# Seven half-size products in place of eight for the first channel product of a token-and-channel mixer

## The chip, the cores and the metric

The kernel runs on one core of one Trainium2 chip. A core has a matrix engine (TensorE, PE in the profile, with the loading of its weights shown apart as PEld), a vector engine (VectorE, DVE), an engine for functions of one argument (ScalarE, ACT), a general engine (GpSimd, POOL) and a queue engine (SyncE, SP), which here only issues transfers. Each engine takes its own instructions in their order; they meet through semaphores. TensorE writes to PSUM, which has eight banks of 512 float32 columns in each of 128 partitions; DVE and ACT read it from there and write to SBUF.

The metric is the device time of one execution in microseconds. The kernel before took 360.32 us (median of three runs, 360.3 to 360.47).

## The reference

For each of 8 batches: attention of 12 heads with a sigmoid in place of the softmax, over 448 tokens with 64 values each, gives x (448 tokens x 768). Then a token mixer and a channel mixer:

```
attn = sigmoid(q @ k.T / 8 - log(448))      # 448 x 448 for each head
x    = attn @ v                             # heads side by side: 448 x 768
h    = relu(x.T @ w_tok1) @ w_tok2          # 768 x 256, then 768 x 448
u    = x + h.T
h2   = relu(u @ w_ch1)                      # 448 x 1536: the first channel product
out  = u + h2 @ w_ch2                       # 448 x 768
```

The first channel product, u @ w_ch1, is the one that is changed: per batch 448 x 768 times 768 x 1536. Inputs and outputs are float32; the kernel multiplies in float16 and accumulates in float32.

## The kernel before, in words

The work is cut in 24 cycles, c = 0 to 23, three to a batch: cycle c = 3b + u computes the scores of unit u of batch b, which is four heads. In a cycle there are seven score steps j. In each, four matmuls with 64 x 64 weights fill one PSUM tile of two banks (L178 to L187, the tag `qk`, two such tiles), and one ACT instruction (L188) puts the sigmoid of both banks into a tile `att`. One cycle later `av` multiplies them with the values (L208) into two banks, and DVE copies these to `xT` (L217, with a small copy at L221 behind it), which holds x transposed. A transfer turns `xT` into `xn` (L232). One cycle after that, `tok_tail` and `tok1` make the first token product (L267, L286; ReLU on ACT, L300) and `ytrans` the second (L307), to which DVE adds x (L314): that gives `ut`, the transposed u, 768 channels in six blocks of 128 partitions with 448 tokens each.

When all three units of a batch are in `ut`, the two channel products follow. The first (`ch1`, L339) works by 12 blocks of 128 output channels: six matmuls of 128 x 128 weights with 448 columns accumulate into one bank, and DVE takes it out with the ReLU (L350) into `h2`. From cycle 9 on all 72 matmuls of batch b - 1 stand in one run near the end of the cycle with u = 2 of batch b, between the last piece of the second channel product of batch b - 2 (L488; DVE adds u and writes out, L513) and `ytrans` (L895 to L901). The second (`ch2_pair`, L362 and L464, with L428 on DVE; `ch2_last`, L488) is spread over the three cycles behind it. Batches 0 and 1 have their own order (L740 to L848). Batch 7's channel products stand after all else (L929).

The order on each engine is that in which the Python code emits the instructions; there is no scheduler. The framework sets the semaphore waits from the tiles that an instruction reads and writes. Four PSUM banks, `m0` to `m3`, are handed out by number (`bank`, L79 to L86; the code sets `at_bank` to choose); the other four are the two `qk` tiles. Tiles in SBUF that share a tag form a ring of `bufs` buffers; a new tile waits until the one that had its buffer is done with.

Beside this run the layouts of q and k for the batches to come: `relayout` copies on DVE (L120) followed by transposing transfers on SP's queue (L133). They are emitted one by one in gaps (`copies`); in a cycle with u = 2 two of them stand on DVE right after L314's additions of the cycle before, and the last two pieces inside the run of `ch1`. Loads on POOL's queue for batch b + 2 are released when the last of these layouts has landed (`gated_loads`, L723 to L732). The un-transposed u (`un`, L321) comes by transfer, too.

The lines that the prediction speaks of are L120, L188, L217, L221, L241 (transposes on TensorE for the first units), L267, L286, L300, L307, L314, L339, L350, L428, L488, L509 (ACT's copy at the very end) and L513.

Of the kernel before, what the change touches and what calls it, by code (L numbers as in the profile page):

```python
# [11 lines left out]
ADD = mybir.AluOpType.add  # L12
MAX = mybir.AluOpType.max
SIGMOID = mybir.ActivationFunctionType.Sigmoid
RELU = mybir.ActivationFunctionType.Relu
# [6 lines left out]
NP = 64  # L22
NU = 3
OPENING_BANKS = "20130130130130213021302130213021313021213021302130202130123102302132132032"


@with_exitstack
def kernel(
# [34 lines left out]
    w1 = pc.tile([128, 4, TT], FP16, name="w1")  # L63
    w2s = pc.tile([128, 2, S], FP16, name="w2s")
    w2 = pc.tile([128, 2, NJ, NP], FP16, name="w2")
# [107 lines left out]
    def qk(b, u, j):  # L173
        if j == 0:
            att[b, u] = pa.tile(
                [128, 2, NJ, S], FP16, tag="att", bufs=2, name=f"att_{b}_{u}"
            )
        ps = pp.tile([128, 2, 512], FP32, tag="qk", bufs=2, name=f"qk_{b}_{u}_{j}")  # L178
        for g in range(2):
            for hi in range(2):  # L180
                nc.tensor.matmul(  # L181
                    out=ps[64 * g : 64 * g + 64, hi, 0:S],
                    lhsT=tr[b, "k"][64 * hi : 64 * hi + 64, u, j, 64 * g : 64 * g + 64],
                    rhs=tr[b, "q"][64 * hi : 64 * hi + 64, u, :, 64 * g : 64 * g + 64],
                    start=True,
                    stop=True,
                )  # L187
        nc.scalar.activation(  # L188
            out=att[b, u][:, :, j, :],
            in_=ps[:, :, 0:S],  # L190
            func=SIGMOID,
            bias=bias_t[:, :],
            scale=att_scale,
        )
# [3 lines left out]
    def av(b, u, j0=0, j1=NJ):  # L198
# [6 lines left out]
        for j in range(j0, j1):  # L205
            for g in range(2):
                for hi in range(2):
                    nc.tensor.matmul(  # L208
                        out=ps[g][64 * hi : 64 * hi + 64, 0:S],
                        lhsT=raw[b, "v"][64 * g : 64 * g + 64, u, hi, j, :],  # L210
                        rhs=att[b, u][64 * g : 64 * g + 64, hi, j, :],
                        start=(j == 0),
                        stop=(j == NJ - 1),
                    )
# [10 lines left out]

    def xn_tile(b):
        if b not in xn:
            xn[b] = pa.tile([128, NU, 2, 4, 128], FP16, tag="xn", bufs=2, name=f"xn_{b}")
        return xn[b]

    def xtrans_dma(b, u):
        nc.sync.dma_start_transpose(  # L232
            out=xn_tile(b)[:, u, :, :, :].rearrange("s g t d -> s (g t) d"),
            in_=xTs[b % 2][:, u, :, :].rearrange("d g s -> d (g s)"),
        )

    def xtrans(b, u):
        ps = bank([128, 4, 2, 128], FP16, f"xb_{b}_{u}")
        for g in range(2):
# [6 lines left out]
        nc.vector.tensor_copy(  # L246
            out=xn_tile(b)[:, u, :, :, :].rearrange("s g t d -> s t g d"),
            in_=ps[:, :, :, :],
# [4 lines left out]
    def h1_tile(b, u):  # L253
        if u == 0:
            h1[b] = pa.tile([128, 2, 2, NU, 128], FP16, tag="h1", bufs=2, name=f"h1_{b}")

    def tok_tail(b, u):
# [6 lines left out]
        for tcb in range(2):  # L264
            part = slice(64 * tcb, 64 * tcb + 64)
            for g in range(2):
                nc.tensor.matmul(  # L267
                    out=tks[b][tcb][64 * g : 64 * g + 64],
                    lhsT=w1[part, 3, 128 * tcb + 64 * g : 128 * tcb + 64 * g + 64],
                    rhs=xn[b][part, u, :, 3, :],  # L270
                    start=True,
# [3 lines left out]
    def tok1(b, u, relu_on_vector=False, with_scores=False):  # L275
# [6 lines left out]
        for tcb in range(2):  # L282
            cols = slice(128 * tcb, 128 * tcb + 128)
            for t in range(3 if with_scores else 4):
# [3 lines left out]
                    lhsT=w1[rows, t, cols],  # L288
                    rhs=xn[b][rows, u, :, t, :],
                    start=(t == 0 and not with_scores),  # L290
                    stop=(t == (2 if with_scores else 3)),
                )
        for tcb in range(2):
            dst, src = h1[b][:, tcb, :, u, :], ps[tcb]
            if relu_on_vector:
# [5 lines left out]

    def ytrans(b, u):
        for g in range(2):
            db = NU * g + u
            ps = bank([128, 512], FP32, f"yt_{b}_{db}")
            for tcb in range(2):
                nc.tensor.matmul(  # L307
                    out=ps[:, 0:S],
                    lhsT=h1[b][:, tcb, g, u, :],
                    rhs=w2[:, tcb, :, :],  # L310
# [59 lines left out]
    def ch1_pair(b, cb):  # L370
# [21 lines left out]
        return turns[0], turns[1], end  # L392

    outs = {}
    orow = out.rearrange("b (p j) d -> b j p d", j=NJ)

    def ch2(b, t, half, n0=0, n1=NCB):
        cols = slice(DH * half, DH * half + DH)
        if n0 == 0:
            if half == 0:  # L400
                outs[b, t] = pa.tile([128, D], FP32, tag="outs", bufs=4, name=f"o_{b}_{t}")
            acc[b] = bank([128, 512], FP32, f"c2_{b}_{t}_{half}")
        ps = acc[b]
        for cb in range(n0, n1):
            nc.tensor.matmul(  # L405
                out=ps[:, 0:DH],
                lhsT=h2[b][:, cb, 128 * t : 128 * t + 128],
                rhs=c2[:, cb, cols],
                start=(cb == 0),
# [33 lines left out]
    def ch2_pair(b, t):  # L443


        outs[b, t] = pa.tile([128, D], FP32, tag="outs", bufs=4, name=f"o_{b}_{t}")
        ps = [bank([128, 512], FP32, f"c2_{b}_{t}_{p}") for p in range(2)]
        n_quads = 8

        def step(turn, n):  # L450
# [3 lines left out]
                turn,  # L454
                lambda p, part, m: h2[b][part, n, 128 * t + m : 128 * t + m + 64],
                lambda p, part: c2[part, n, DH * p : DH * p + DH],
                n == 0,
# [3 lines left out]
        def rest():  # L461
            for p in range(2):
                for n in range(n_quads, NCB):
                    nc.tensor.matmul(  # L464
                        out=ps[p][:, 0:DH],
                        lhsT=h2[b][:, n, 128 * t : 128 * t + 128],
                        rhs=c2[:, n, DH * p : DH * p + DH],
                        start=False,
# [7 lines left out]
    def ch2_last(b, n0=0, n1=NCB):  # L476
# [9 lines left out]
        for n in range(n0, n1):  # L486
            for g in range(2):
                nc.tensor.matmul(  # L488
                    out=ps[g],
                    lhsT=h2[b][:, n, 384:448],  # L490
                    rhs=c2[:, n, DH * g : DH * g + DH],
                    start=(n == 0),
# [4 lines left out]
        for n in range(NU if add_on_pe else 0):  # L497
            for g in range(2):
# [6 lines left out]
                )  # L505
        o = pa.tile([128, DH], FP32, tag="outl", bufs=2, name=f"o_{b}_3")
        for g in range(2):
# [232 lines left out]
    for c, cb in ((N_FIRST, 3), (N_FIRST + 1, 8)):  # L740
# [44 lines left out]
        else:  # L785
# [9 lines left out]
            gated_loads(b)  # L795

    pending, copies = [], []
    for c in range(2 * NU, ONE_RUN):
        b, u = divmod(c, NU)
# [12 lines left out]
        def work(share):  # L812
            goal = 3 * sum(shares[: c - first]) + share * shares[c - first]
            done = 0
            while pending and spent + done < total * goal / 90:
# [3 lines left out]
                if copies:  # L819
                    copies.pop(0)()  # L820
            return done

# [23 lines left out]
        if u == 2:  # L846
            gated_loads(b)
    assert not copies and not pending  # L848

    for c in range(ONE_RUN, N_CYCLES):  # L850
# [17 lines left out]
        if u == 2:  # L868
            utrans(b - 1)
        at_bank[0] = Y  # L870
        av(*before, 0, 4)
# [50 lines left out]
    for f in work[20:24]:  # L922
        f()
    ytrans(*ahead)
    ytrans(*before)
    utrans(B - 1)
    for f in work[24:]:
        f()
    for w, f in stage2(B - 1):  # L929
        f()  # L930
# [30 lines left out]
```

## Time and profile before

| what | value |
|---|---|
| device time, median of three | 360.32 us (360.3 to 360.47) |
| the profiled execution: span from first to last instruction | 358.7 us |
| what lies around the span (median less span; the profile gives no device time of its own) | 1.6 us |
| PE busy | 351.7 us, 98% |
| DVE busy | 184.7 us, 51% |
| ACT busy | 169.5 us, 47% |
| PE in line L339 (`ch1` without the first pair of each start batch) | 108.2 us, 552 matmuls |
| DVE in line L350 (ReLU of `ch1`) | 59.5 us, 96 instructions |
| HBM read, written | 43.45 MB, 11.01 MB |

A row of the table of groups reads: line, engine, operation, output<-input by the program's names, shapes, count, busy time and mean duration of one in ns, idle time of the engine just before these instructions and what ended it. A row of the timeline reads: start in us from the begin of the span, length in us from the first to the last end, engine, line, operation, names, shape, count, and in brackets the idle time before and what ended it. Matmuls overlap in the engine, so the length of a run of n matmuls is n - 1 times the distance between starts plus the duration of one.

### The profile page before, as it was taken

The numbers are of one execution on the slowest core, as the hardware profiler recorded it, in microseconds if no ns is written. First come the engines' busy times: TensorE is split into PE (matmuls) and PEld (weight loads), VectorE is DVE, ScalarE is ACT, GpSimd is POOL, SyncE is SP. The second block draws the span as 40 slices with busy tenths as digits, with TensorE's granted clock in tenths as the row PEclk, the third lists the DMA queues.
The fourth block names the chain that finished last, engine by engine and source line by source line (L and its number), as shares of the span: only waits on it lengthen the run. The fifth ranks groups of instructions, "written<-read, shape, count | busy, mean of one in ns | idle before, by whom it ended". The sixth has DMA issues, their size and how long they took to land.

```text
span 358.7 us, 9225 instructions
## 1 busy us (share of the span) xinstructions
PE 351.7 (98%) x4099; PEld 204.3 (57%) x4099; DVE 184.7 (51%) x343; ACT 169.5 (47%) x215; POOL 56.3 (16%) x98
## 2 busy tenths in 40 slices
PE   7999999999999999999999999999999999999995
PEld 4555565555456655666556655666456655555553
DVE  2376558247455555454645655455553445516521
ACT  3996844675458810787038820777028830010000
POOL 8974330220120004000040004000010000000000
PEclk9999999999999999999999999999999999999999
DMA  7999999999998797959989597949963680047014
GB/s 122 175 176 198 205 204 196 164 203 234 186 176 153 115 199 133 206 96 195 186 125 185 121 202 128 207 94 149 227 88 75 104 155 0 13 106 141 14 46 110
DMA packets 104375, 52.11 MB, mean 145 GB/s; under 512 B 76432, under 2 KB 101264, under 8 KB 104336
## 3 DMA queue, kind: packets, MB, share of 16 engines
q1 hardware_dynamic: 78944, 29.70, 46.0%
q0 software_dynamic: 25168, 21.50, 39.0%
q8 instruction: 32, 0.52, 0.6%
q10 hardware_dynamic: 224, 0.33, 0.4%
q14 instruction: 7, 0.06, 0.0%
HBM read 43.45 MB, written 11.01 MB: 152 GB/s over the span
## 4 chain that ended last, share of the span: by engine, by line
PE 92%; ACT 4%; DMA 1%; DVE 1%; issue 0%; DVEq 0%; ACTq 0%
PE c L339 30%; PE c L362 12%; PE c L405 10%; PE qk L181 10%; PE xa L208 8%; PE tk L286 6%; PE c L464 5%; PE yt L307 5%; PE c L488 5%; ACT att L188 4%; DMA first_q<-in_q_dram 1%; PE tp_k L161 1%; PE tp_q L161 1%; PE tk L267 1%; PE heat L626 0%; DVE ut L314 0%
## 5 line engine op out<-in xcount | busy, mean ns | idle before, releaser
L188 ACT ACTIVATE att<-qk,att_bias 128x896 f16<-128x896 f32 x168 | 154.7, 1016 | 114.3 <-PE qk L181 114.2
L339 PE MATMUL c<-ut,c 128*128 128x448 f16 x552 | 108.2, 353 | 0.0
L339 PEld LDWEIGHTS <-c 128*128 128x128 f16 x552 | 52.5, 98 | 52.3 <-issue 3.5
L350 DVE TENSOR_SCALAR h<-c 128x448 f16<-128x448 f32 x96 | 59.5, 624 | 43.6 <-PE c L339 42.0
L181 PE MATMUL qk<-tr_q,tr_k 64*64 64x448 f16 x672 | 57.9, 359 | 0.2
L428 DVE TENSOR_TENSOR o<-un,c 128x384 f32<-128x384 f16 x42 | 23.3, 554 | 49.7 <-PE c L464 28.1
L217 DVE CAST xT<-xa 128x448 f16<-128x448 f32 x48 | 27.7, 620 | 40.3 <-PE xa L208 40.3
L362 PE MATMUL c<-c,h 64*64 64x384 f16 x960 | 46.6, 323 | 0.0
L208 PE MATMUL xa<-att,raw_v 64*64 64x448 f16 x672 | 39.6, 349 | 0.0
L405 PE MATMUL c<-c,h 128*128 128x384 f16 x216 | 37.5, 326 | 0.0
L362 PEld LDWEIGHTS <-h 64*64 64x64 f16 x960 | 28.1, 107 | 11.8
L181 PEld LDWEIGHTS <-tr_k 64*64 64x64 f16 x672 | 21.2, 105 | 20.1 <-issue 12.3
L300 ACT ACTIVATE h<-tk 128x256 f16<-128x256 f32 x42 | 14.4, 417 | 33.4 <-PE tk L286 33.4
L405 PEld LDWEIGHTS <-h 128*128 128x128 f16 x216 | 20.5, 98 | 14.4 <-issue 1.4
L314 DVE TENSOR_TENSOR ut<-xT,yt 128x448 f16<-128x448 f16 x48 | 27.4, 614 | 2.6 <-PE yt L307 2.5
L725 POOL COPY gate<-tr_q 128x2 f16<-128x2 f16 x6 | 1.1, 184 | 170.4 <-DMA tr_q<-rel_q 170.4
L208 PEld LDWEIGHTS <-raw_v 64*64 64x64 f16 x672 | 20.4, 107 | 11.0 <-issue 0.7
L464 PE MATMUL c<-c,h 128*128 128x384 f16 x120 | 22.0, 326 | 0.0
L307 PE MATMUL yt<-w,h 128*128 128x448 f16 x96 | 21.9, 353 | 0.0
L286 PE MATMUL tk<-xn,w 128*128 128x256 f16 (+1 forms) x156 | 21.8, 274 | 0.1
L286 PEld LDWEIGHTS <-w 128*128 128x128 f16 (+1 forms) x156 | 13.4, 98 | 7.4 <-issue 5.2
L488 PE MATMUL c<-c,h 128*64 128x384 f16 x192 | 17.3, 328 | 0.0
(58 smaller groups left out, 195.0 us busy)
## 6 DMA issues: line engine op xcount, KB each, us to landing
out_dram<-o SPq DMA_DIRECT2D x48, 192.0 KB, 3.1
c<-in_moe_w_ch_dram POOLq DMA_DIRECT2D x4, 1152.0 KB, 15.3
raw_k<-in_k_dram POOLq DMA_DIRECT2D x10, 336.0 KB, 7.2
raw_q<-in_q_dram POOLq DMA_DIRECT2D x10, 336.0 KB, 10.5
raw_v<-in_v_dram POOLq DMA_DIRECT2D x10, 336.0 KB, 5.5
out_dram<-o SPq DMA_DIRECT2D x15, 96.0 KB, 2.3
raw_q<-in_q_dram POOLq DMA_DIRECT2D x12, 112.0 KB, 5.7
raw_k<-in_k_dram POOLq DMA_DIRECT2D x12, 112.0 KB, 5.7
```

The costliest lines, as they stand in the source:

```text
L181: nc.tensor.matmul(out=ps[64 * g : 64 * g + 64, hi, 0:S], lhsT=tr[b, "k"][64 * hi : 64 * hi + 64, u, j, 64 * g : 64 * g + 64], rhs=tr[b, " ...
L188: nc.scalar.activation(out=att[b, u][:, :, j, :], in_=ps[:, :, 0:S], func=SIGMOID, bias=bias_t[:, :], scale=att_scale,)
L208: nc.tensor.matmul(out=ps[g][64 * hi : 64 * hi + 64, 0:S], lhsT=raw[b, "v"][64 * g : 64 * g + 64, u, hi, j, :], rhs=att[b, u][64 * g : 64 ...
L217: nc.vector.tensor_copy(out=xTs[b % 2][:, u, g, 0:S], in_=ps[g][:, 0:S])
L286: nc.tensor.matmul(out=ps[tcb], lhsT=w1[rows, t, cols], rhs=xn[b][rows, u, :, t, :], start=(t == 0 and not with_scores), stop=(t == (2 if ...
L307: nc.tensor.matmul(out=ps[:, 0:S], lhsT=h1[b][:, tcb, g, u, :], rhs=w2[:, tcb, :, :], start=(tcb == 0), stop=(tcb == 1),)
L339: nc.tensor.matmul(out=ps[:, 0:S], lhsT=c1[:, BY_UNIT[d], 128 * cb : 128 * cb + 128], rhs=uts[b % 2][:, BY_UNIT[d], 0:S], start=(d == 0), ...
L350: nc.vector.tensor_scalar(out=h2[b][:, cb, :], in0=ps[:, 0:S], scalar1=0.0, scalar2=None, op0=MAX)
L362: nc.tensor.matmul(out=ps[p][m : m + 64, 0:n], lhsT=lhsT(p, part, m), rhs=rhs(p, part), start=(first and turn == 0), stop=(last and turn = ...
L405: nc.tensor.matmul(out=ps[:, 0:DH], lhsT=h2[b][:, cb, 128 * t : 128 * t + 128], rhs=c2[:, cb, cols], start=(cb == 0), stop=(cb == NCB - 1 ...
L464: nc.tensor.matmul(out=ps[p][:, 0:DH], lhsT=h2[b][:, n, 128 * t : 128 * t + 128], rhs=c2[:, n, DH * p : DH * p + DH], start=False, stop=(n ...
L488: nc.tensor.matmul(out=ps[g], lhsT=h2[b][:, n, 384:448], rhs=c2[:, n, DH * g : DH * g + DH], start=(n == 0), stop=(n == NCB - 1 and not ad ...
```

## The change

The first channel product of batches 2 to 7 is no longer computed as 72 matmuls of 448 columns. u.T is cut in channels (low and high half, blocks 0 to 2 and 3 to 5) and tokens (first and second 224), w_ch1 in input channels (low and high) and output channels (first and second 768). The product of 2 x 2 blocks with 2 x 2 blocks is then made from seven products of blocks in place of eight, with sums of blocks of the weights made once (`weight_sums`) and sums of blocks of u made for each batch (`token_sums`).

A step of `ch1_seven` is named by the product's number, 1 to 7, and a letter: a, b, c are three groups of output channels, each of two blocks of 128 in the first half and the two that answer to them in the second. A step is six matmuls of 128 x 128 weights with 224 columns: three input blocks, for each of the two output blocks side by side in one bank. Products 1, 6, 7 and 4 accumulate one on the other in the same bank ("place 0"); after 1 and after 6 ACT copies the sum so far to a float32 tile `parts`, after 7 DVE adds `parts` to it, after 4 ACT takes the ReLU. Products 5 and 3 share "place 1" (ACT copies after 5, DVE adds after 3), product 2 has "place 2" (DVE adds). Each addition on DVE is followed by a second DVE instruction that takes the maximum with 0 in place in `h2`.

Places 0 and 1 of group a are the two banks of one `qk` tile, those of group b the two banks of the other; group c has three of the banks `m`, and place 2 is a bank `m` in all groups. The steps stand in the order of `SEVENS`, 20 of them, then `ytrans`, then 4c. In batch 7 the order is that of `last`, with the first half of the first group of `ch2` in place of `ytrans`.

The sums of weights, nine DVE instructions of 768 columns, are put between the matmuls of cycle 6; three more, which write over a quarter of c1, stand in cycle 9 after `rest`. `token_sums`, four DVE instructions of 672 columns, stand at the begin of each cycle with u = 2, behind `utrans` and ahead of `av`.

To make room in SBUF: `w2s` and `first_q` share a ring with `parts`; `att` becomes a ring of 11 tiles of one score step each in place of two tiles of seven; `xn` a ring of 3 tiles and `h1` of 2 tiles of one unit, in place of two tiles of three; `outs` has 3 buffers for 4, `outl` 1 for 2. `ch2` reads `h2` by groups (`BY_GROUP`).

```diff
+BY_GROUP = [0, 1, 6, 7, 2, 3, 8, 9, 4, 5, 10, 11]
...
-    first_q = pc.tile([128, 2, NJ, E], FP32, name="first_q")
+    w2s = pa.tile([128, 2, S], FP16, tag="parts", bufs=2, name="w2s")
+    first_q = pa.tile([128, 2, NJ, E], FP32, tag="parts", bufs=2, name="first_q")
+    sums = [pc.tile([128, NU, CC // 2], FP16, name=f"sum{n}") for n in (1, 2, 4)]
+    diffs = pc.tile([128, 4, NU, NS], FP16, name="diffs")
...
     def qk(b, u, j):
-        if j == 0:
-            att[b, u] = pa.tile(
-                [128, 2, NJ, S], FP16, tag="att", bufs=2, name=f"att_{b}_{u}"
-            )
+        att[b, u, j] = pa.tile([128, 2, S], FP16, tag="att", bufs=11, name=f"att_{b}_{u}_{j}")
...
+    def weight_sums():
...
+        def one(out, in0, in1, op):
+            return [
+                lambda d=d: nc.vector.tensor_tensor(
+                    out=out[:, d, :], in0=in0[:, d, :], in1=in1[:, d, :], op=op
+                )
+                for d in range(NU)
+            ]
+
+        return [
+            *one(s1, c1[:, high, second], c1[:, low, second], ADD),
+            *one(s2, s1, c1[:, low, first], SUB),
+            *one(s4, c1[:, high, first], s2, SUB),
+        ], one(c1[:, low, second], c1[:, low, first], c1[:, low, second], SUB)
+
+    def token_sums(b, u0=0, u1=NU):
...
+        for out, in0, in1, op in (
+            (t1, ut[:, k1, n2], ut[:, k1, n1], SUB),
+            (t3, ut[:, k2, n2], ut[:, k1, n2], SUB),
+            (t2, t3, ut[:, k1, n1], ADD),
+            (t4, ut[:, k2, n1], t2, SUB),
+        ):
+            nc.vector.tensor_tensor(out=out, in0=in0, in1=in1, op=op)
+
+    def ch1_seven(b, banks):
...
+                    if (at[0],) not in held:
+                        held[(at[0],)] = pp.tile(
+                            [128, 2, 512], FP32, tag="qk", bufs=2, name=f"c7_{b}_{at[0]}"
+                        )
+                    held[g, which] = held[(at[0],)][:, at[1], :]
+            return held[g, which][:, 0:S].rearrange("c (p n) -> c p n", p=2)
+
+        def step(n, g):
+            which = {1: 0, 6: 0, 7: 0, 4: 0, 5: 1, 3: 1, 2: 2}[n]
+            ps = place(g, which)
+            for d in range(NU):
+                for p in range(2):
+                    cols = slice(128 * (2 * g + p), 128 * (2 * g + p) + 128)
+                    nc.tensor.matmul(
+                        out=ps[:, p, :],
+                        lhsT=weights[n][:, d, cols],
+                        rhs=moving[n][:, d, :],
+                        start=(n in (1, 5, 2) and d == 0 and p == 0),
+                        stop=(d == NU - 1 and p == 1),
+                        skip_group_check=True,
+                    )
+            if n == 1:
+                parts[g] = pa.tile([128, 3, 2, NS], FP32, tag="parts", bufs=2, name=f"pt_{b}_{g}")
+            part = parts[g]
+            top, bottom = (slice(c, c + 2) for c in (2 * g, 2 * g + NCB // 2))
+            if n in (1, 6, 5):
+                at = {1: 0, 6: 1, 5: 2}[n]
+                nc.scalar.activation(out=part[:, at, :, :], in_=ps, func=COPYF)
+            elif n == 4:
+                nc.scalar.activation(out=h2[b][:, bottom, n1], in_=ps, func=RELU)
+            else:
...
+                nc.vector.tensor_tensor(out=dst, in0=part[:, at, :, :], in1=ps, op=ADD)
+                nc.vector.tensor_scalar(
+                    out=dst, in0=dst, scalar1=0.0, scalar2=None, op0=MAX
+                )
...
+    SEVENS = [
+        (int(x[0]), "abc".index(x[1]))
+        for x in "1a 5a 1b 6a 5b 2a 6b 7a 3a 2b 7b 4a 3b 1c 4b 5c 2c 6c 3c 7c".split()
+    ]
...
         if u == 2:
             utrans(b - 1)
+            token_sums(b - 1)
         at_bank[0] = Y
         av(*before, 0, 4)
...
         rest()
+        while late:
+            late.pop(0)()
...
-            at_bank[0] = Y
-            for n, (w, f) in enumerate(pieces_ch1(b - 1)):
-                f()
-                if copies and n % 2 == 1:
-                    copies.pop(0)()
-        at_bank[0] = Y
-        ytrans(*ahead)
+            step = ch1_seven(
+                b - 1, [(("q", 0), ("q", 1), 0), (("r", 0), ("r", 1), 2), (1, 3, 0)]
+            )
+            for at, (n, g) in enumerate(SEVENS):
+                step(n, g)
+                if copies and at % 2 == 1:
+                    copies.pop(0)()
+            ytrans(*ahead, (2, 0))
+            step(4, 2)
...
-    for w, f in stage2(B - 1):
+    token_sums(B - 1, 2, NU)
...
+    last = "1a 2a 1b 2b 5a 6a 5b 6b 7a 3a 7b 4a 3b 1c 4b 5c 2c 6c 3c 7c".split()
+    for x in last:
+        step(int(x[0]), "abc".index(x[1]))
+    at_bank[0] = m[1]
+    ch2(B - 1, 0, 0, 0, 6)
+    step(4, 2)
+    at_bank[0] = m[2]
+    ch2(B - 1, 0, 0, 6, NCB)
```

More of the change, by code (lines that the diff above doesn't have):

```diff
@@ L188, in qk @@
         nc.scalar.activation(
-            out=att[b, u][:, :, j, :],
+            out=att[b, u, j][:, :, :],
             in_=ps[:, :, 0:S],
@@ L392, in ch1_pair @@
         return turns[0], turns[1], end
+    MC = CC // 2
+    def weight_sums():
+        low, high = slice(0, NU), slice(NU, NDB)
+        first, second = slice(0, MC), slice(MC, CC)
+        s1, s2, s4 = sums
+        def one(out, in0, in1, op):
[10 more added lines that the diff above has]
+        ], one(c1[:, low, second], c1[:, low, first], c1[:, low, second], SUB)
@@ L847 @@
             gated_loads(b)
-    assert not copies and not pending
+    assert not copies and not pending and not early
     for c in range(ONE_RUN, N_CYCLES):
@@ L924 @@
     ytrans(*ahead)
+    token_sums(B - 1, 0, 2)
     ytrans(*before)
@@ L928 @@
         f()
-    for w, f in stage2(B - 1):
+    token_sums(B - 1, 2, NU)
+    at = at_bank[0]
+    m = [(at + n) % 4 for n in range(4)]
+    step = ch1_seven(
+        B - 1, [(("q", 0), ("q", 1), m[0]), (("r", 0), ("r", 1), m[1]), (m[2], m[3], m[0])]
+    )
+    last = "1a 2a 1b 2b 5a 6a 5b 6b 7a 3a 7b 4a 3b 1c 4b 5c 2c 6c 3c 7c".split()
[6 more added lines that the diff above has]
+    ch2(B - 1, 0, 0, 6, NCB)
+    for t, half in groups[1:]:
+        for n in range(0, NCB, 3):
+            ch2(B - 1, t, half, n, n + 3)
+    for w, f in pieces_last(B - 1):
         f()
```

101 lines of the change are left out of this document (75 added, 26 removed).

## The prediction

> **What bounds the kernel now.** I read the page's busy times and slices first, then the chain that ended last, the groups, and then the timeline around one run of the first channel product (129 to 144 us) for what each engine does there.
>
> ```profile
> PE 351.7 (98%) x4099; PEld 204.3 (57%) x4099; DVE 184.7 (51%) x343; ACT 169.5 (47%) x215; POOL 56.3 (16%) x98
> ...
> PEclk9999999999999999999999999999999999999999
> ...
> PE 92%; ACT 4%; DMA 1%; DVE 1%; issue 0%; DVEq 0%; ACTq 0%
> ...
> L120 DVE COPY rel_k<-raw_k 128x896 f16<-128x896 f16 x17 | 10.0, 611 | 1.2 <-DMA raw_k<-in_k_dram 1.2
> L221 DVE COPY xT<-xT 128x128 f16<-128x128 f16 x20 | 3.9, 195 | 0.7
> ```
>
> TensorE is the bound from end to end, at full granted clock: matmul columns taken away are worth their time, and any wait of PE costs its length. The timeline rows:
>
> ```profile
> 18.21 0.62 PE L241 MATMUL xb<-ident,xT 128*128 128x128 f16 x8
> 157.59 0.83 PE L286 MATMUL tk<-xn,w 128*128 128x256 f16 x6
> 129.16 13.96 PE L339 MATMUL c<-ut,c 128*128 128x448 f16 x72
> 142.96 0.92 PE L307 MATMUL yt<-w,h 128*128 128x448 f16 x4
> 143.81 0.57 PE L181 MATMUL qk<-tr_q,tr_k 64*64 64x448 f16 x8
> 130.46 0.87 PEld L339 LDWEIGHTS <-c 128*128 128x128 f16 x6 [0.43 <-DVE o L513]
> 144.31 2.80 ACT L188 ACTIVATE att<-qk,att_bias 128x896 f16<-128x896 f32 x3 [17.32 <-PE qk L181]
> 354.45 0.55 DVE L511 COPY o<-c 64x384 f32<-64x384 f32 x1 [1.68 <-PE c L499]
> 354.49 0.48 ACT L509 ACTIVATE o<-c 64x384 f32<-64x384 f32 x1 [32.68 <-PE c L499]
> 161.82 1.14 DVE L120 COPY rel_q<-raw_q 128x896 f16<-128x896 f16 x2
> 164.02 1.16 DVE L217 CAST xT<-xa 128x448 f16<-128x448 f32 x2 [1.06 <-PE xa L208]
> 165.49 0.28 PE L267 MATMUL tk<-xn,w 64*64 64x256 f16 x4
> ```
>
> To be seen: matmuls with 128 x 128 weights start 56 ns apart at 128 columns (L241), 109 at 256 (L286), 189 at 448 (L339), each with a weight load of its own. ACT has nothing to do for 17 us around the run. At 130.46 a matmul waits for DVE to free its bank (L513): its start comes 345 instead of 189 ns after the one before. So a wait of PE on a bank is paid in full.
>
> **The columns.** At 224 columns the line between 56 and 109 gives 95.8 ns. Per batch 72 x 189.2 = 13.62 us become 126 x 95.8 = 12.07 us: -1.55, six times: **-9.3**. The stall at 130.46 (0.155; the bank of `ch2_last` is not used again until 1c) goes from five batches: **-0.8**.
>
> **The waits, where I differ from what the edit looks like.** In the changed program as built, each instruction names the count that it waits for. The first matmul of 5a waits for ACT's copy after 1a; 6a for the copy after 5a; 5b after 1b; 6b after 5b; 3a for DVE's addition after 7a; 4a after 3a; 3b after 7b; 4b after 3b. 5a writes another bank than 1a, but both are halves of one `qk` tile, and the wait is set by the tile. Group c has a tile per bank and waits only where a bank is used again.
>
> Prices: a step is 6 x 95.8 = 0.575 us. Its last result comes 0.16 after the step's end (a matmul's duration at 224 columns, 0.26 between the rows' 0.22 and 0.27, less 0.096). ACT starts 0.05 later (0.04 at L300's, 0.07 at L509's first after idling), needs 0.54 (L509's 0.485 for 384 columns, ACT's 0.8 ns per column for 64 more), and PE starts 0.05 after it (at 54.01 us, after a sigmoid's end). So **0.80** from the end of a step to the start of one that waits for its copy. With DVE: 0.16 + 0.04 + 0.62 (L350, L314) + 0.06 = **0.88**. A second DVE instruction, the maximum, follows each addition 0.03 later (as L221 behind L217) and holds DVE for m. No row has it. It can't be shorter than L221's 128 columns (0.195 long, 0.11 to the next start) and not longer than the same operation from PSUM (L350, 0.54). The float16 copies L221 and L120 give 0.29 on the line between them; L221 has the nearer shape (two short rows), so I take 0.24. An addition with its maximum holds DVE for 0.89.
>
> Stalls of PE per batch, in the order of `SEVENS`: 5a 0.80 (nothing between); 6a 0.80 - 0.575 (1b) = 0.23; 6b 0.23; 3a 0.88; 3b: 7b's addition stands behind those of 3a and 2b: 0.20 + 0.89 + 0.89 + 0.62 + 0.06 - 3 x 0.575 (2b, 7b, 4a) = 0.94; 4b 0.88 - 0.575 = 0.30; 7c behind 6c's copy 0.23; 4c behind 7c's and 3c's additions, less `ytrans` (0.76), 0.23. Sum 3.84; eight restarts cost about 0.02 each (the start after a stall comes 200 rather than 189 ns before the next), and a second wait on an instruction 0.06 once. **4.0** per batch, five times: **+20.0**.
>
> Batch 7, in its order: 6a 0.81, 6b 0.81, 3a 0.88, 4a 0.30, 3b 0.32, 4b 0.30, 7c 0.23, then 0.16 before the blocks that 4c's ReLU on ACT delivers (0.80 less four matmuls of 162 ns), restarts 0.1: **+3.9**.
>
> **Token sums.** In a cycle with u = 2 DVE is done with L120 at 162.9 and idles to 164.02. Four additions of 672 float16 columns follow now, two of them behind a result just written (+0.1). No row shows a two-input float16 addition in SBUF: at L120's two elements a cycle 0.41 each, at the one a cycle of L314 0.77. I take 0.41, because L120's operands are also all float16 in SBUF. Then 1.86 us, L217 starts at 164.76, its second copy frees bank 1 at 165.92, and L267's second pair, started at 165.50 now, waits: +0.48. In batches 3 to 6: **+1.9**; the cycle of batch 7 has no L120 there and covers them.
> The Trainium skill, VectorE: DVE Perf Modes, section on the perf-mode tier table, has a two-input addition of 16-bit operands in SBUF at twice the base rate and a scalar operation at four times. By the first the sums stay at 0.41; by the second m is near 0.18 and the whole about 1 us less. L120's copy runs at two a cycle, not four, so the trace bears that out only in part.
>
> **Late and early sums.** In cycle 9 three additions of 768 columns (0.46 each) stand ahead of L314 (111.07 before), whose banks `av` needs at 113.14: the second comes free at 113.6, **+0.5** (0 if `av` had slack, 1.7 at one a cycle). The nine in cycle 6 lie in DVE's idle time of 66.9 to 73.5 us (4.2 us of work beside 1.1): nothing; without that cover they would delay `av` of the next cycle.
>
> **What else moves, at no cost.** ACT's twelve instructions per batch lie in its 17 us. The sigmoids now wait twice each; ACT is behind PE's scores by most of a cycle, so that the 0.06 hides. Rings: with 11 `att` tiles score step j waits for the `av` of 11 steps ago, which stands ahead of it on PE in every cycle; `xn`, `h1`, `outs` are free a cycle or more before (an output lands in 3.1 us). SP's and POOL's queues keep their order. If L120's last copy came late, the loads would, but they gain slack with a slower kernel.
>
> **Sum.** -9.3 - 0.8 + 20.0 + 3.9 + 1.9 + 0.5 = +16.2 on the span of 358.7, so 374.9, and 1.6 around it as in the median: **376.5 us**. Bounds: m at 0.11 gives -2.0, both sums hidden -2.4, so 372; m at 0.54 gives +5. The likeliest case spans 371 to 383.
>
> **The rivals.**
> 1. *The waits do not hold PE* (faster). If each bank counted alone, only 4b (0.1), 7c and 4c (0.23 each) would wait: 0.6 per batch and 0.4 in batch 7. Then -9.3 - 0.8 + 3.4 + 2.4 = -4.3: **356.0**. For it: ACT is idle and DVE half idle there. Against it: the counts named in the program, and the stall at 130.46. It decides at 1.3 us of waiting per batch (10.1 of gain, 2.4 for the sums, six batches); I count 4.0.
> 2. *Two-input additions run at one element a cycle.* The token sums then cost 1.9 per batch instead of 0.48 (+5.7), the late ones +1.2, and the nine of cycle 6 overrun their cover by about 2: **385**. Against it: L120's rate.
> 3. *Weight loads set the pace.* If one load had to end before the next began, 126 loads at the row's 98 ns would be 12.35 us, +0.28 in six batches: **378**. Against it: L241, where loads of 128 columns follow each other in 56 ns. The Trainium skill, TensorE: Matmul & The Clock Gate, section on LDWEIGHTS, gives 1/1.2 ns per weight column, an estimate of 107 ns; by that the whole would be about 385, and L241 disagrees.
>
> **How the numbers follow.** Forecast 0.80, rival 1 0.05, rival 2 0.08, rival 3 0.04, others 0.03. Four cases of five lie in 371 to 383, which is the range. A measurement of this kernel tells 0.2% (0.7 us) from no change; only rival 1 and half of the others are faster: 0.06 faster, 0.01 the same, 0.93 slower.
>
> **What would show it.** Per batch, 16.9 us from 1a to the next scores where 14.65 stood; idle time of PE ahead of the new matmuls, ended by ACT after 1a, 5a, 5b and by DVE after 7a and 7b, none of it in 1b or 2b; matmuls 96 ns apart within a step; PE's share down to about 95%. Wrong, if 5a follows 1a without a gap, if the maximum takes longer than 0.4, or if L267 in the u = 2 cycles isn't late.

## The result, and the profile after

The changed kernel takes **375.84 us** (median of 4 runs, 375.44 to 376.34) where the kernel before takes 360.31 (359.72 to 360.47): a ratio of 1.0433, 95% interval 1.0419 to 1.0448. It is 4.3% slower, with an eighth less matmul work in the stage that was changed. The profiled execution of the changed kernel has a span of 374.0 us and a time of 375.81, so 1.8 lies around the span.

The page of the changed kernel has busy times, the granted clock, the chain by engine, and a group of section 5:

```profile
PE 350.1 (94%) x4423; PEld 235.9 (63%) x4423; DVE 204.6 (55%) x419; ACT 208.7 (56%) x287; POOL 56.4 (15%) x98
...
PEclk9999999999999999999999999999999999999999
...
PE 72%; DVE 13%; DMA 6%; ACT 3%; issue 2%; POOL 2%; DVEq 0%; ACTq 0%; POOLq 0%
...
L503 DVE TENSOR_TENSOR h<-pt,c 128x448 f16<-128x448 f32 x30 | 18.5, 618 | 25.9 <-ACT pt L494 21.9
```

PE's busy time fell by only 1.6 us and not by 9.3: the page counts a matmul as busy for its whole duration of 0.26, so that ahead of every stall 0.16 us more are counted that lay under the next matmul before. The share fell from 98% to 94%, with a span that is 15.3 us longer. The clock is full in every slice. The chain that ended last, 92% PE before, now runs 13% through DVE and 3% through ACT: PE waits for them. Its 6% of DMA lie in the opening, in the first loads and before L341's wait for its weights at 33 us; that costs nothing by the time the change begins, as the scores of cycle 6 start at 63.56 us here and at 63.74 before. The list of waits says for what (total us, times, longest us):

```profile
PE c_q L480 <- DVE h L503: 4.7, 6, 0.8
PE c_q L480 <- ACT pt L494: 3.8, 6, 0.6
PE c_r L480 <- DVE h L503: 3.3, 5, 0.7
...
PE tk L267 <- DVE xT L219: 0.9, 4, 0.2
...
PE c_r L480 <- ACT pt L494: 0.6, 1, 0.6
```

All four rows on L480 name a matmul of the seven products that writes `c_q` or `c_r`, the two `qk` tiles in whose halves groups a and b are put. These figures count from the end of the last matmul's 0.26 and so show 0.16 less per wait than PE loses; a wait of 0.22 leaves next to nothing in this list, and none of group c's is in it. What PE loses is read from start to start, against the pitch of 0.096 us. So I read one run, that of 130 to 147 us, from the timeline of the changed kernel (start, length, instruction; in brackets the idle time before it and what ended it):

```profile
130.10 0.75 PE L480 MATMUL c_q<-ut,c 128*128 128x224 f16 x6
130.89 0.54 ACT L494 ACTIVATE pt<-c_q 128x448 f32<-128x448 f32 x1 [3.20 <-PE c_q L480]
131.49 0.73 PE L480 MATMUL c_q<-diffs,sum 128*128 128x224 f16 x6 [0.63 <-ACT pt L494]
132.06 0.74 PE L480 MATMUL c_r<-ut,c 128*128 128x224 f16 x6
...
136.89 0.73 PE L480 MATMUL c_q<-ut,sum 128*128 128x224 f16 x6 [0.78 <-DVE h L503]
...
137.66 0.62 DVE L503 TENSOR_TENSOR h<-pt,c_q 128x448 f16<-128x448 f32 x1 [0.52 <-PE c_q L480]
138.31 0.28 DVE L504 TENSOR_SCALAR h<-h 128x448 f16<-128x448 f16 x1
138.51 0.61 DVE L503 TENSOR_TENSOR h<-pt,c 128x448 f16<-128x448 f32 x1
139.16 0.28 DVE L504 TENSOR_SCALAR h<-h 128x448 f16<-128x448 f16 x1
139.35 0.61 DVE L503 TENSOR_TENSOR h<-pt,c_r 128x448 f16<-128x448 f32 x1
140.02 0.74 PE L480 MATMUL c_r<-ut,sum 128*128 128x224 f16 x6 [0.67 <-DVE h L503]
...
146.79 0.57 PE L183 MATMUL qk<-tr_q,tr_k 64*64 64x448 f16 x8
```

1a starts at 130.10, ACT's copy runs from 130.89 to 131.43, and 5a, which writes the other half of the same tile and doesn't need the copy, starts at 131.49 instead of 130.68. 3a (136.89) and 3b (140.02) stand behind DVE in the same way; before 3b one sees DVE's queue, three additions and two maxima one behind the other. 1b at 132.06 follows 5a after 0.57 with no gap. From 1a to the next scores it is 16.69 us, where 14.65 stood.

### The profile page after: what moved, and what is told of

Read it like the earlier page. It is cut to its first block, busy times and chain, and to the rows that moved or that the text cites. A ratio compares the mean times of both kernels' runs of the same rounds, so it can differ in the third digit from the quotient of the medians.

```text
span 374.0 us, 10172 instructions
## 1 busy us (share of the span) xinstructions
PE 350.1 (94%) x4423; PEld 235.9 (63%) x4423; DVE 204.6 (55%) x419; ACT 208.7 (56%) x287; POOL 56.4 (15%) x98
## 4 chain that ended last, share of the span: by engine, by line
PE 72%; DVE 13%; DMA 6%; ACT 3%; issue 2%; POOL 2%; DVEq 0%; ACTq 0%; POOLq 0%
PE c L521 10%; PE c L364 8%; PE qk L183 7%; PE c_q L480 6%; PE c L341 6%; PE xa L210 6%; PE c_r L480 5%; PE c L582 5%; PE c L480 5%; DVE h L503 5%; PE tk L286 5%; PE c L606 4%; DMA c<-in_moe_w_ch_dram 3%; ACT pt L494 3%; PE yt L309 2%
## 5 line engine op out<-in xcount | busy, mean ns | idle before, releaser
L183 PE MATMUL qk<-tr_q,tr_k 64*64 64x448 f16 x672 | 59.0, 357 | 0.4 <-DVE tr_k L175 0.2
L544 DVE TENSOR_TENSOR o<-un,c 128x384 f32<-128x384 f16 x42 | 23.3, 554 | 49.9 <-PE c L582 29.3
L219 DVE CAST xT<-xa 128x448 f16<-128x448 f32 x48 | 27.7, 619 | 34.7 <-PE xa L210 34.7
L480 PEld LDWEIGHTS <-c 128*128 128x128 f16 x432 | 41.0, 98 | 7.5 <-issue 6.9
L480 PEld LDWEIGHTS <-sum 128*128 128x128 f16 x324 | 31.1, 97 | 17.8 <-issue 17.8
L364 PEld LDWEIGHTS <-h 64*64 64x64 f16 x960 | 28.9, 107 | 11.3
L503 DVE TENSOR_TENSOR h<-pt,c 128x448 f16<-128x448 f32 x30 | 18.5, 618 | 25.9 <-ACT pt L494 21.9
L494 ACT ACTIVATE pt<-c_q 128x448 f32<-128x448 f32 x18 | 9.8, 543 | 28.2 <-PE c_q L480 28.2
L341 PE MATMUL c<-ut,c 128*128 128x448 f16 x120 | 24.6, 353 | 0.9 <-DMA c<-in_moe_w_ch_dram 0.9
L300 ACT ACTIVATE h<-tk 128x256 f16<-128x256 f32 x42 | 14.2, 408 | 16.2 <-PE tk L286 16.2
L309 PE MATMUL yt<-w,h 128*128 128x448 f16 x96 | 21.9, 353 | 0.0
L286 PE MATMUL tk<-xn,w 128*128 128x256 f16 (+1 forms) x156 | 21.8, 274 | 0.1
```

The lines of the kernel that those rows point to most:

```text
L183: nc.tensor.matmul(out=ps[64 * g : 64 * g + 64, hi, 0:S], lhsT=tr[b, "k"][64 * hi : 64 * hi + 64, u, j, 64 * g : 64 * g + 64], rhs=tr[b, " ...
L219: nc.vector.tensor_copy(out=xTs[b % 2][:, u, g, 0:S], in_=ps[g][:, 0:S])
L286: nc.tensor.matmul(out=ps[tcb], lhsT=w1[rows, t, cols], rhs=xn[b, u][rows, :, t, :], start=(t == 0 and not with_scores), stop=(t == (2 if ...
L309: nc.tensor.matmul(out=ps[:, 0:S], lhsT=h1[b, u][:, tcb, g, :], rhs=w2[:, tcb, :, :], start=(tcb == 0), stop=(tcb == 1),)
L341: nc.tensor.matmul(out=ps[:, 0:S], lhsT=c1[:, BY_UNIT[d], 128 * cb : 128 * cb + 128], rhs=uts[b % 2][:, BY_UNIT[d], 0:S], start=(d == 0), ...
L364: nc.tensor.matmul(out=ps[p][m : m + 64, 0:n], lhsT=lhsT(p, part, m), rhs=rhs(p, part), start=(first and turn == 0), stop=(last and turn = ...
```

## The experiments

Two theories were to be told apart. Mine: PE waits because two products at once live in the halves of one tile, and a matmul into one half is held until the other engine has read the other half. The rival: seven products give ACT and DVE, with eighteen copies, additions and maxima more per batch, more than they can do beside PE, wherever the products lie.

### e1_banks: other places, same steps

```diff
-  [(("q", 0), ("q", 1), 0), (("r", 0), ("r", 1), 2), (1, 3, 0)]
+  [(("q", 0), 3, 2), (("r", 0), 0, 2), (1, 3, 2)]
...
-  [(("q", 0), ("q", 1), m[0]), (("r", 0), ("r", 1), m[1]), (m[2], m[3], m[0])]
+  [(("q", 0), m[2], m[0]), (("r", 0), m[3], m[1]), (m[2], m[3], m[0])]
```

> The changed kernel with the same twenty-one steps, copies, additions and maxima in the same order; only the PSUM places differ, so that no two places in use at once are halves of one `qk` tile (group a: half 0 of its tile and two single banks, group b likewise, group c three single banks). Theory (PE waits because two halves of a tile are released as one): the waits of 5a 0.79, 6a and 6b 0.22, 3a 0.95, 3b 0.83 and most of 4b's 0.30 go; 7c's 0.22 and 4c's 0.24 stay, since both are on one bank used again. Of 3.77 us a batch some 0.5 is left, which saves 5 x 3.3 in batches 2 to 6 and about 3.4 in batch 7: 375.8 - 19.9 = 356 us (354.5 to 357.5), below the kernel before. Rival (seven products give ACT and DVE more than they can do in the time, and PE waits for them whatever the banks): 374 to 376.

Measured: 357.6 us (356.78 to 358.18), 0.9903 of before (0.9867 to 0.9939), span of the profile 355.0. With these two lists of numbers alone, 18 us come back. The end of the same run, with the two stalls that are left in it (timeline of e1_banks; 4b waits another 0.02):

```profile
140.83 0.64 PE L480 MATMUL c<-ut,sum 128*128 128x224 f16 x5
...
141.53 0.74 PE L480 MATMUL c<-diffs,c 128*128 128x224 f16 x6
...
141.88 1.34 POOL L114 DMA_DIRECT2D raw_k<-in_k_dram  x2
...
142.10 0.92 PE L309 MATMUL yt<-w,h 128*128 128x448 f16 x4
142.23 0.44 DVE L504 TENSOR_SCALAR h<-h 128x448 f16<-128x448 f16 x1
142.59 0.60 DVE L503 TENSOR_TENSOR h<-pt,c 128x448 f16<-128x448 f32 x1
...
143.24 0.73 PE L480 MATMUL c<-diffs,c 128*128 128x224 f16 x6 [0.22 <-DVE h L503]
143.91 0.57 PE L183 MATMUL qk<-tr_q,tr_k 64*64 64x448 f16 x8
```

7c (141.53) starts 0.32 after the matmul before it, so it waits 0.22 as expected. 4c (143.24) waits 0.39 here, in one other batch 0.42 and in three 0.24, the value expected. In the rows the difference is the maximum at 142.23, which takes 0.44 instead of 0.28 and holds up the addition that 4c waits for; the last section says what lies beside it. The profile's span fell by 19.0 us where 19.9 was expected; the median lies 1.6 above the forecast and 0.1 above its range. The run takes 13.55 us (130.36 to 143.91) against 16.69 and, before the change, 14.65. The rival is out: ACT and DVE do the same work in 3.1 us less.

### e7_order: same places, another order

If the wait is as I think, it can also be filled. With the changed kernel's own places, other steps are put between a copy and the next step on that tile:

```diff
-  "1a 5a 1b 6a 5b 2a 6b 7a 3a 2b 7b 4a 3b 1c 4b 5c 2c 6c 3c 7c"
+  "1a 5b 5a 1b 6a 2b 6b 3a 2a 7b 7a 1c 2c 5c 3b 6c 3c 4a 7c 4b"
```

A group's `parts` tile is now made at the group's first step, whichever product that is; here 5b comes before 1b.

> The changed kernel with its own PSUM places, halves of one tile for two products at once, and the sums where they were; only the order of the steps in batches 2 to 6 differs (1a 5b 5a 1b 6a 2b 6b 3a 2a 7b 7a 1c 2c 5c 3b 6c 3c 4a 7c 4b, `ytrans`, 4c). Theory (the wait is for the last use of the tile by another engine, at 0.80 us for ACT and 0.88 for DVE, and what PE has to do in between is taken off): of 3.77 us a batch two waits of 0.24 (5a and 6a) stay, so five times -3.3: 375.8 - 16.4 = 359.5 us, batch 7 unchanged (359 to 361). Rival (what e1_banks gained came from keeping PE and ACT out of the same tile, not from the order): 374 to 376.

Measured: 360.58 us (359.71 to 363.79, 10 runs), 1.0007 of before (0.9985 to 1.0029): 15.3 of the 16.4 us expected, with PE and ACT still in halves of the same tiles. So it isn't sharing a tile that costs, but coming back to it too early. The profiled execution is the longest of the ten runs (363.79). It lost time in the opening (the last section has the figures) and 1.1 us in cycle 13, where L267 waits for the transfer of `xn`; inside a run of the seven products it can be read. Its timeline:

```profile
134.25 0.73 PE L480 MATMUL c_q<-diffs,sum 128*128 128x224 f16 x6
134.83 0.73 PE L480 MATMUL c_r<-ut,c 128*128 128x224 f16 x6
135.62 0.73 PE L480 MATMUL c_q<-diffs,sum 128*128 128x224 f16 x6
...
139.64 1.31 PE L480 MATMUL c<-ut,c 128*128 128x224 f16 x12
...
140.98 0.61 DVE L503 TENSOR_TENSOR h<-pt,c_q 128x448 f16<-128x448 f32 x1
...
141.71 0.98 ACT L494 ACTIVATE pt<-c 128x448 f32<-128x448 f32 x2 [3.62 <-DVE h L503]
...
142.30 0.73 PE L480 MATMUL c<-diffs,sum 128*128 128x224 f16 x6 [0.20 <-ACT pt L494]
```

5a (134.25) and 6a (135.62) wait 0.22 each, as expected. The third stall, 0.36 at 6c (142.30), I had not expected. It comes from a ring, not from a bank: group c's `parts` tile takes the place of group a's, so ACT's copies of 1c and 5c wait until DVE has done its last addition of group a (140.98 to 141.59). ACT stood still for 3.62 us. For most of that it had nothing to copy; the last result of 1c comes at 140.38 (0.575 + 0.16 behind 139.64), so the ring held the copy for 1.3, and 6c waited for it. In the five batches this stall is 0.36, 0.10, 0.35, 0.10 and 0.10, together 1.0 us, and 15.3 came back where 16.4 were expected. Whether L267's wait for `xn` is in the other nine runs, no profile shows.

### e4_halves: the wait by itself, in the kernel before

The kernel before, with its 448-column products, and the output blocks of the first product taken in pairs in the two halves of a `qk` tile:

```diff
+            if b > 1:
+                if cb % 2 == 0:
+                    pair[0] = pp.tile([128, 2, 512], FP32, tag="qk", bufs=2, ...)
+                acc[b, cb] = pair[0][:, cb % 2, :]
+            else:
                 acc[b, cb] = bank([128, 512], FP32, f"c1_{b}_{cb}")
```

> The kernel before, with one thing changed: from batch 2 on two neighbouring output blocks of the first channel product are put in the two halves of one `qk` tile instead of in two single banks. The arithmetic, the matmuls and their order are the same. Theory (a wait holds for the tile and not for the bank): the matmuls of each odd block wait for DVE's ReLU of the even block, about 0.16 + 0.04 + 0.62 + 0.06 = 0.88 us each; six per batch in six batches are +31.7, less the stall of 0.155 in five of them: about 391 us. Rival (each half counts alone): 359.5 to 360.3.

Measured: 393.04 us as the median of two runs (391.17 and 394.92), 1.0886 of before (1.0818 to 1.0954). The profiled execution, 391.17, has a span of 389.4, 30.7 more than before; 31.7 - 0.8 = 30.9 was expected. Its list of waits and its timeline:

```profile
PE c L344 <- DVE h L355: 25.8, 36, 0.7
```

```profile
131.19 2.43 PE L344 MATMUL c<-ut,c 128*128 128x448 f16 x12 [0.71 <-DVE h L355]
132.52 0.62 DVE L355 TENSOR_SCALAR h<-c 128x448 f16<-128x448 f32 x1 [0.86 <-PE c L344]
133.66 0.62 DVE L355 TENSOR_SCALAR h<-c 128x448 f16<-128x448 f32 x1 [0.51 <-PE c L344]
134.34 2.43 PE L344 MATMUL c<-ut,c 128*128 128x448 f16 x12 [0.71 <-DVE h L355]
```

36 waits: one for each odd block, six in each of six batches. From one odd block to the next it is 3.15 us (131.19 to 134.34), where twelve matmuls take 2.27: 0.88 per wait, the price that the forecast gave a wait for DVE. The effect is there without any of the change's arithmetic.

### e2_sums: the sums elsewhere in DVE's queue

```diff
         if u == 2:
             utrans(b - 1)
-            token_sums(b - 1)
         at_bank[0] = Y
         av(*before, 0, 4)
+        if u == 2:
+            token_sums(b - 1)
...
-        while late:
-            late.pop(0)()
...
             ytrans(*ahead)
+        while late:
+            late.pop(0)()
```

> The changed kernel with two things moved in the program's order, nothing else: the token sums of a cycle with u = 2 come behind the first half of `av` (so behind the copies of L217 on DVE) instead of ahead of it, and the three late weight sums of cycle 9 come behind `ytrans` instead of ahead of L314. Theory (the sums hold up a copy that PE's next matmuls wait for): L267 late by 0.39 in four cycles and `av` by 0.34 in cycle 9 go, -1.9 us: 373.9. Rival (the lost time only shows up at the next wait of the cycle, or the sums now delay the first steps of the seven products): 375.8, no change.

Measured: 373.68 us (373.21 to 373.88), 1.0347 of before (1.0314 to 1.0379): 2.2 us less than the changed kernel, where 1.9 was expected. The same place in both timelines, first the changed kernel, then e2_sums:

```profile
165.88 0.92 DVE L430 TENSOR_TENSOR diffs<-ut 128x672 f16<-128x672 f16 x2
...
167.79 1.15 DVE L219 CAST xT<-xa 128x448 f16<-128x448 f32 x2
168.49 0.28 PE L267 MATMUL tk<-xn,w 64*64 64x256 f16 x2
169.00 0.30 PE L267 MATMUL tk<-xn,w 64*64 64x256 f16 x2 [0.23 <-DVE xT L219]
```

```profile
166.47 1.16 DVE L219 CAST xT<-xa 128x448 f16<-128x448 f32 x2 [1.06 <-PE xa L210]
167.76 0.92 DVE L430 TENSOR_TENSOR diffs<-ut 128x672 f16<-128x672 f16 x2
167.94 0.28 PE L267 MATMUL tk<-xn,w 64*64 64x256 f16 x4
```

In the first, L219 stands behind the sums and L267 comes in two pairs with 0.51 between them; in the second L219 follows its product, DVE idles 1.06 before it, and the four matmuls stay together. The time didn't come back elsewhere. Read by stage it is 2.65: each of the four cycles is 0.52 shorter (26.82 to 26.30 from its scores to the next) and cycle 10 is 0.55 shorter, while the opening of e2_sums' profile is 0.5 longer.

### e3_rings: the storage alone

The kernel before, with the ring sizes and tags of the change and the full product:

```diff
-  att[b, u] = pa.tile([128, 2, NJ, S], FP16, tag="att", bufs=2, ...)
+  att[b, u, j] = pa.tile([128, 2, S], FP16, tag="att", bufs=11, ...)
...
-  xn[b] = pa.tile([128, NU, 2, 4, 128], FP16, tag="xn", bufs=2, ...)
+  xn[b, u] = pa.tile([128, 2, 4, 128], FP16, tag="xn", bufs=3, ...)
...
-  h1[b] = pa.tile([128, 2, 2, NU, 128], FP16, tag="h1", bufs=2, ...)
+  h1[b, u] = pa.tile([128, 2, 2, 128], FP16, tag="h1", bufs=2, ...)
```

> The kernel before, with the full first product in every batch, and only the storage of the change: a tile of `att` per score step in a ring of 11, a tile of `xn` and of `h1` per cycle in rings of 3 and 2, three `outs`, one `outl`, and `w2s` and `first_q` in the `parts` ring. Theory (as forecast, the rings cost nothing): 360.3, within 0.2% of before. Rival (shorter rings hold up the sigmoids, the transposes or the output copies): up to 1 us or more above before, with new waits of ACT or DVE.

Measured: 360.37 us, 0.9990 of before (0.9959 to 1.0020), span 358.5 against 358.7. Within what the measurement can tell, an interval of 0.4% below to 0.2% above, these rings cost nothing.

### e5_best and e6_last: what the identity is worth without its waits

e5_best joins the places of e1_banks, the sums of e2_sums, and this order in batches 2 to 6 (with `parts` made at a group's first step, as in e7_order):

```diff
-  "1a 5a 1b 6a 5b 2a 6b 7a 3a 2b 7b 4a 3b 1c 4b 5c 2c 6c 3c 7c"
+  "1b 5a 1a 2b 6b 6a 3a 5b 2a 7a 7b 1c 3b 5c 6c 2c 4b 7c 3c 4a"
```

> The changed kernel with the places of e1_banks, the sums where e2_sums has them, and in batches 2 to 6 another order of the steps (1b 5a 1a 2b 6b 6a 3a 5b 2a 7a 7b 1c 3b 5c 6c 2c 4b 7c 3c 4a, `ytrans`, 4c), in which at least two steps lie between every copy or addition and the step that writes its bank again. Theory (a wait costs PE only what is left of 0.80 or 0.88 us after the steps between): the 0.22 of 7c and the 0.39 of 4c that are left per batch in e1_banks go, five times -0.6, and the sums' -1.9 as in e2_sums: 357.6 - 3.0 - 1.9 = 352.7, about 2% under the kernel before; range 351 to 353.5. Rival (ACT or DVE has no room left once PE waits no more, so that new waits appear further on): 354 to 357.

Measured: **351.67 us** (350.89 to 352.07), 0.9739 of before (0.9718 to 0.9759), 2.6% faster and inside the range expected. The timeline of e5_best:

```profile
129.63 0.75 PE L480 MATMUL c_r<-ut,c 128*128 128x224 f16 x6
130.21 0.74 PE L480 MATMUL c<-diffs,sum 128*128 128x224 f16 x6
130.79 0.74 PE L480 MATMUL c_q<-ut,c 128*128 128x224 f16 x6
...
135.86 0.61 DVE L503 TENSOR_TENSOR h<-pt,c_q 128x448 f16<-128x448 f32 x1
135.96 0.74 PE L480 MATMUL c<-ut,c 128*128 128x224 f16 x6
136.51 0.28 DVE L504 TENSOR_SCALAR h<-h 128x448 f16<-128x448 f16 x1
...
136.78 0.54 ACT L494 ACTIVATE pt<-c 128x448 f32<-128x448 f32 x1 [1.80 <-DVE h L504]
...
141.89 0.74 PE L480 MATMUL c<-diffs,c 128*128 128x224 f16 x6
142.56 0.57 PE L183 MATMUL qk<-tr_q,tr_k 64*64 64x448 f16 x8
```

From 1b to the next scores 12.94 us without a stall, 1.71 less than before: 1.55 of columns and the 0.155 of the old stall, to the hundredth what the forecast had taken. ACT's wait of 1.80 us before the copy of 1c is not the ring's here: 7a's addition, the last to read group a's tile, ends at 136.47, and the last result of 1c comes only at 136.70. (The row names a maximum of L504, but that ends at 136.79, no earlier than the copy begins.) One wait is new further on, though not the rival's, of ACT or DVE: L267 waits once for the transfer of `xn`, and cycle 13 takes 8.83 us for 8.30. In the profile of e1_banks that cycle takes 8.41, in those of e6_last and e7_order 8.93 and 9.42.

e6_last has another order in batch 7 as well:

```diff
-  "1a 2a 1b 2b 5a 6a 5b 6b 7a 3a 7b 4a 3b 1c 4b 5c 2c 6c 3c 7c"
+  "1a 2a 1b 2b 5a 6a 5b 6b 7a 3a 7b 4a 1c 3b 4b 6c 5c 2c 7c 3c"
...
-  ch2(B - 1, 0, 0, 0, 6)
+  ch2(B - 1, 0, 0, 0, 4)
   step(4, 2)
...
-  ch2(B - 1, 0, 0, 6, NCB)
+  ch2(B - 1, 0, 0, 4, NCB)
```

> e5_best with another order in batch 7 as well (1a 2a 1b 2b 5a 6a 5b 6b 7a 3a 7b 4a 1c 3b 4b 6c 5c 2c 7c 3c, then four blocks of the first group of the second product, 4c, and the other eight). In batch 7 of e1_banks 7c waits 0.22 and the blocks behind 4c 0.15. Theory: both go, 0.37 us less than e5_best, about 0.1%. Rival: they come back at 3b or 4c, no difference.

Measured: 351.65 us (350.49 to 354.83), 0.9752 of before (0.9715 to 0.9789). The medians can't tell it from e5_best. In the profiles the stretch from 1a of batch 7 to the last group of the second product takes 23.94 us (319.81 to 343.75) against 24.29 (319.40 to 343.69): 0.35 less, where 0.37 was expected.

## Why the prediction was right

The sign, the place and the mechanism were as forecast, and the time (376.5 us) was 0.7 us too long. Its terms, with what the profile of the changed kernel has in their place:

| term of the sum | forecast | measured | read from |
|---|---|---|---|
| columns, six batches | -9.3 | -9.3 | steps 0.575 apart; e5_best's run |
| the stall at the second matmul | -0.8 | -0.8 | e5_best's run |
| waits, batches 2 to 6 | +20.0 | +18.75 | 5 x (16.69 - 12.94) |
| waits, batch 7 | +3.9 | +3.8 | starts in that batch |
| token sums | +1.9 | +2.1 | four cycles: first L267 to L286 0.92 for 0.40 us |
| late weight sums | +0.5 | +0.55 | scores of cycles 10 to 11: 8.86 for 8.30 us |
| sum | +16.2 | +15.1 | spans: 374.0 - 358.7 = +15.3 |

The 0.2 that is left over isn't assigned. From cycle 6 on it is 0.4, as the opening of the changed kernel's profile is 0.2 shorter, and most of that lies behind the last scores. So the 0.7 us by which the forecast was too long are 1.35 too much in the waits, less 0.25 in the two kinds of sums, 0.2 that isn't assigned and 0.2 more around the span (1.8 for 1.6): that it came so near is in part luck.

The single waits, in us beyond the pitch of the matmuls:

| | 5a | 6a | 6b | 3a | 3b | 4b | 7c | 4c |
|---|---|---|---|---|---|---|---|---|
| forecast | 0.80 | 0.23 | 0.23 | 0.88 | 0.94 | 0.30 | 0.23 | 0.23 |
| measured | 0.79 | 0.22 | 0.22 | 0.95 | 0.83 | 0.30 | 0.22 | 0.24 |

They sum to 3.77 where the forecast had 3.84 and 0.22 more for restarts and a second wait. 3a has the second wait in it: the addition after 7a starts 0.10 after the last result instead of 0.04. Most of what was too large are the restarts, 0.16 a batch: after a stall the next starts of these 224-column matmuls are 95 ns apart, no more than elsewhere, where I had taken 11 ns over from 448 columns and rounded up. Run against run, e5_best without stalls and the changed kernel with them, the loss is 3.75 a batch and not 4.0. That is the term that was mis-sized, by 1.25 us in five batches.

3b was the wait with the most terms in it, and its error is the maximum's hold on DVE: 0.20 (138.31 to 138.51) where I took 0.24 from float16 copies. Two of them stand ahead of 7b's addition. The row that was missing before is L504's, 448 float16 columns from SBUF to SBUF in 0.28, with 0.20 to the next start. At the 0.51 ns per column that the additions of L430 show below, 448 columns alone would be 0.23, so the maximum goes faster than that rate. This agrees with the four-times tier that the Trainium skill, VectorE: DVE Perf Modes, section on the perf-mode tier table, gives a scalar operation. The copy is the poorer neighbour for it. The sign of being wrong, a maximum longer than 0.4, shows in five of the 54 (0.44 to 0.55), but the stalls are the same in those batches to 0.01.

The other rivals. Rival 1 had 356.0 if each bank counted alone; e1_banks, where each does, takes 357.6, so the reckoning was sound to 1.6 us and its condition false. Rival 2 (additions at one element a cycle): L430's additions of 224, 448 and 672 columns take 0.272, 0.384 and 0.500, which is 0.51 ns per column. Additions that read float32 from PSUM are slower: 384 columns (L544) take 0.554 and 448 (L503) 0.618, which is 1.0 ns per column. The same table of the Trainium skill has two-input 16-bit additions at twice the base rate, and these rows agree. Each addition of 672 columns was 0.09 longer than the 0.41 assumed, but they overlap, and from the first start to L219 it is 1.91 us for 1.86. Rival 3 (weight loads set the pace): 126 loads of 128 columns go through in 12.1 us of steps, 0.096 each. An estimate of 107 ns per load from the Trainium skill, TensorE: Matmul & The Clock Gate, section on LDWEIGHTS, does not hold as a pace here.

*What the forecast lacked.* It priced the rings that existed before and got them right (e3_rings), but it didn't look at the new one: the two `parts` tiles for three groups. In the changed kernel it costs nothing, as PE is late anyway; in e7_order it makes a stall of its own, and in e5_best none. The transfers it looked at for a slower kernel alone; in the faster one `xn` came late once. And it said nothing of what the identity would be worth with other places or another order. Every number for that was in it: -10.1 for columns and the old stall, of which e5_best keeps 8.4 by the spans (358.7 to 350.3).

## What to carry to other kernels

A faster product is worth its columns only if PE doesn't return to a tile that another engine has still to read: count, for each accumulator, the time from its last matmul to the end of its reader (here 0.80 us with ACT, 0.88 with DVE), and what PE has to do in between. Two accumulators that are halves of one tile count as one in that reckoning, so give each its own tile, or put two steps of other work between them; here the first was worth 18 us, the second 15, and both together, with a better place for two small sets of additions, made of 4.3% slower 2.6% faster. When a stage is cut short, look through each queue that it adds work to (DVE's, here) for a small instruction that PE's next matmul stands behind.

## What I had not expected of the hardware

- PE loses almost nothing beyond the wait itself: eight stalls that sum to 3.77 us cost a run 3.75, and the starts behind a stall are 95 ns apart like the others.
- The maximum (L504) is sometimes longer, and each time beside a DMA that POOL issues. It takes 0.276 to 0.279 us, except that 14 of the 162 in the profiles of the changed kernel, e1_banks and e5_best take 0.36 to 0.55. Each of those lies over a DMA that POOL issues (L114), starts 0.23 to 0.38 us after that began, and ends 0.07 to 0.10 us after its end; no maximum without such an issue beside it is longer than 0.279. The additions (L503), which read PSUM, show nothing of it: the 27 that overlap an issue in these profiles take 0.60 to 0.62. So the same instruction takes up to twice as long. In e1_banks' rows it is the one at 142.23, over the issue that began at 141.88, and such a maximum stands ahead of 4c in both batches where 4c waits 0.39 and 0.42 instead of 0.24. The Trainium skill, SBUF — State Buffer, section on SBUF's two separate sides, has DVE and GpSimd share a pair of ports that one of them holds alone, DVE when it runs in a mode that uses both ports; the rows agree in that the loser stands still, though here it is so only for a part of POOL's instruction (maxima that start up to 0.21 us after the issue began, or from 0.46 on, run free). No run takes the issues away, so it is seen together, not shown by trial.
- The opening can shift the whole program between profiles of kernels that do the same work there: the scores of cycle 6 start at 63.56 to 64.20 us in eight of them, and at 66.32 in e7_order's. There L341 waits 1.9 us for its weights (0.9 in the changed kernel; the kernel before has no such wait), and right behind that wait the granted clock is down: 0.70 in the mean of 34 to 38 us and 0.87 from 38 to 42, where the changed kernel has 1.00. In that stretch the 448-column matmuls of L341 and L309 start 373 ns apart instead of 189. The missing clock is 0.30 and 0.13 of 4 us each, 1.7 us, and with the 0.96 of longer waiting that is nearly all of the 2.76 between the two profiles. A difference of a few tenths between two profiles is better read from one stage than from the spans.
